# A quarter of the Q projection as seven-product runs on shared row sums, with the PSUM ring turned by two

## The chip, the cores and the metric

One core of one Trainium2 chip. The time is device time in microseconds (us), the median of several executions. "Before" is the kernel as it stood, "after" the changed one. A profile is taken of one of the executions, and stage times are read from it.

In this kernel TensorE makes the matrix products. A product lies in a bank of PSUM (128x512 floats) until ScalarE or VectorE has read it, and the program waits for these reads before it writes the bank again. A transfer between memories is called a DMA; a queue holds those that one engine has issued.

## The reference

```python
def _A_ref(x, wqkv, wo):                    # B, S, D = 1, 2048, 1024; 32 heads of 32
    q, k, v = ...(x @ wqkv)
    phi = lambda t: jnp.where(t > 0, t + 1, jnp.exp(t)) + 1e-6
    pq, pk = phi(q), phi(k)
    kv = jnp.einsum("bhsd,bhse->bhde", pk, v)
    z = jnp.einsum("bhsd->bhd", pk)
    num = jnp.einsum("bhqd,bhde->bhqe", pq, kv)
    den = jnp.einsum("bhqd,bhd->bhq", pq, z)[..., None] + 1e-6
    return (num / den)... @ wo
def _B_ref(x, w1, b1, w2, b2):              # mixes over the rows: w1 2048x3584, w2 3584x2048
    ...
h = x + _A_ref(_layernorm(x), A_wqkv, A_wo)
h2 = h + _B_ref(_layernorm(h), B_w1, B_b1, B_w2, B_b2)
```

The change lies in `_A_ref`, which the kernel finishes at about 234 us. The rest, the two mixers of `_B_ref`, it doesn't touch.

## The kernel before

The row-normalised x is kept transposed in `xnT` (8 k tiles of 128 partitions). K and V are made in runs that cover two row tiles each. A run takes a 2x2 block product by seven block products (`p1` to `p7`) instead of eight. It needs sums of x blocks (`x_sums`, shared by the K and the V run of the same rows) and of weight blocks (`w_sums`, made once). The runs interleave, so that VectorE and ScalarE work on one while TensorE makes the next.

```python
def x_sums(q):
    a11, a12, a21, a22 = x_blocks(q)
    sm = spool.tile([P, 4, hk2, P], FP16, tag="xs", name="xs")      # two buffers
    pin(nc.vector.tensor_tensor(sm[:, 0], a21, a22, ALU.add))
    ...
class Run:
    def mm(self, ps, lhs, rhs, start):
        for k in range(hk2):                                        # 4 matmuls of 512 columns
            pin(nc.tensor.matmul(ps[:], lhsT=lhs[:, k, :], rhs=rhs[:, k, :], ...))
    def p7(self):
        self.mm(self.C, self.s3, self.t3, False)
        self.add(1, self.C)          # VectorE reads psC
    def p4(self):
        self.mm(self.C, self.a22, self.t4, False)   # TensorE goes on in psC
        self.evac(1, self.C)
    ...
def run_step(n, prev, ...):          # the next run's products between the last run's
    n.p1(); ...; prev.p3(); ...; prev.p4(); n.p6(); ...; n.p2(); n.p5(); ...
```

Q is made in plain units of 8 matmuls of 512 columns, 32 of them. Eight lie between the runs, the other 24 in the "held" stage, beside the folding of `kv` into `wo`, the denominators and the first sums of mixer 1. A denominator row is inverted by ScalarE into a buffer `rd` and sent through DRAM, to be spread over partitions.

```python
q_units = [(u, j) for u in range(NSC) for j in range(ND)]           # 4 x 8
def den_inv(u, ps):
    rd = a3d.tile([P, SW], FP16, tag="rd", name="rd")               # one buffer
    hs.activation(ps[:], ps[:], ACT.Ln, bias=eps_den[:], scale=1.0 / S)
    hs.activation(rd[:], ps[:], ACT.Exp, scale=-1.0)                # hs: ScalarE
    hd.dma_start(rd_dram[u][:], rd[:])
...
for n, (u, j) in enumerate(q_units[8:]):
    q_held(u, j)
    if 4 <= n < 4 + ND:
        fold(n - 4)
    if j == 1:                                                      # every 8 units
        den(u - 1)
        den_spread(u - 1)
    ...
```

Plain units, folds and output tiles take their PSUM bank in turn from a ring of five:

```python
acc_ring[:] = [acc, pool, acc, pool, pool][0:2 + bufs]
def acc_tile():
    acc_ring.append(acc_ring.pop(0))
    return acc_ring[-1].tile([P, BANK], F32, tag="acc", name="acc_t")
```

## Time and profile before

| | before |
|---|---|
| median (range), 3 runs | 560.21 us (560.14 to 560.31) |
| span of the profiled execution | 558.3 us |
| first V run to held stage | 100.46 us |
| held stage, 24 Q units | 47.40 us |
| output stage, up to mixer 1 | 55.90 us |
| mixer 1 to the end | 324.4 us |

The stage lengths are differences of four starts in the timeline of TensorE of the kernel before (start us, length us, engine, line, operation, out<-in, tile, count). They are the first product of the first V run, the first held Q unit, the first output tile and the first product of mixer 1:

```profile
30.11 1.03 PE L946 MATMUL psA<-wkv,xnT 128*128 128x512 bf16 x4
...
130.57 1.67 PE L230 MATMUL acc_t<-xnT,wq_sb 128*128 128x512 bf16 x7
...
177.97 2.32 PE L230 MATMUL acc_t<-wo_sb,pqT 128*128 128x512 f16 x10
...
233.87 2.32 PE L230 MATMUL psA<-hE,wq 128*128 128x512 f16 x10
```

(The end of the span is read to 0.1 us.)

### The profile page before, as it was taken

Reading aid. Unit: us, or ns where it says so; the run is one execution under the profiler, and the core shown is the slowest. Engines: PE = TensorE matmul, PEld = TensorE weight load, DVE = VectorE, ACT = ScalarE, POOL = GpSimd, SP = SyncE. Lnnn points to the kernel's source line nnn. Section 1 sums busy time; section 2 is a strip of 40 time slices with the busy share of each in tenths; the row PEclk is TensorE's granted clock in tenths of the full one; section 3 lists DMA queues with packets and bytes.
Section 4 is the critical chain, followed back from the end, with each engine's and each line's share of the span. In section 5 each row is a group of like instructions: output and inputs, shape, how many; then the busy total and the mean of one; then the engine's idle time right before and its main releaser. Section 6 shows DMA issues by size and latency. Waiting matters only on the chain.

```text
span 558.3 us, 8814 instructions
## 1 busy us (share of the span) xinstructions
PE 551.9 (99%) x3323; PEld 315.8 (57%) x3339; DVE 436.1 (78%) x850; ACT 291.0 (52%) x617; POOL 26.3 (5%) x36
## 2 busy tenths in 40 slices
PE   8999999999999999999999999999999999999997
PEld 3444444454444444456766767667444667767665
DVE  7898888544777688889989889897996878749746
ACT  5747677766767877645455565464310312413312
POOL 1000000000000000000000000000003103103111
PEclk9999999999999999999999999999999999999999
DMA  9933342115764772102240430413769649849434
GB/s 300 304 75 76 82 89 39 19 39 201 224 202 138 239 205 76 75 1 79 75 150 3 150 126 26 151 40 94 197 209 236 195 125 244 214 129 239 93 108 73
DMA packets 83915, 74.51 MB, mean 133 GB/s; under 512 B 15634, under 2 KB 76320, under 8 KB 83872
## 3 DMA queue, kind: packets, MB, share of 16 engines
q1 hardware_dynamic: 79104, 69.61, 41.9%
q0 software_dynamic: 4096, 3.68, 4.8%
q10 hardware_dynamic: 672, 0.66, 0.3%
q8 instruction: 26, 0.43, 0.3%
q14 instruction: 17, 0.14, 0.1%
HBM read 59.12 MB, written 11.67 MB: 127 GB/s over the span
## 4 chain that ended last, share of the span: by engine, by line
PE 95%; DMA 2%; DVE 2%; issue 1%; ACT 0%; DVEq 0%
PE psI L230 25%; PE acc_t L230 18%; PE psC L230 16%; PE psB L230 8%; PE psC L946 4%; PE psB L946 4%; PE psA L946 4%; PE psB L342 2%; PE psA L342 2%; PE acc_t L1232 2%; PE psE L946 2%; DMA x_sb<-in_A_x_dram 2%; PE psC L342 2%; PE acc_t L870 2%; PE psA L230 1%; PE kvps L899 1%
## 5 line engine op out<-in xcount | busy, mean ns | idle before, releaser
L230 PEld LDWEIGHTS <-is 128*128 128x128 f16 x736 | 71.9, 98 | 31.1 <-DVE hi L230 0.4
L230 PEld LDWEIGHTS <-sa 128*128 128x128 f16 x606 | 59.2, 98 | 27.1
L230 PEld LDWEIGHTS <-wq 128*128 128x128 bf16 (+1 forms) x496 | 48.5, 98 | 28.1 <-issue 1.0
L230 PE MATMUL acc_t<-wo_sb,pqT 128*128 128x512 f16 x256 | 55.6, 379 | 0.0
L488 POOL DMA_DIRECT2D out_dram<-wq x28 | 24.4, 928 | 519.8 <-ACT wq L491 489.5
L230 PE MATMUL acc_t<-xnT,wq_sb 128*128 128x512 bf16 x188 | 43.1, 379 | 0.2
L230 PEld LDWEIGHTS <-pqT 128*128 128x128 bf16 x256 | 25.0, 98 | 30.5 <-issue 0.6
L193 DVE TENSOR_SCALAR e_sb<-e_sb 128x512 bf16<-128x512 bf16 x64 | 18.6, 290 | 28.7 <-ACT e_sb L189 28.2
L230 DVE TENSOR_TENSOR t<-psI,t 128x256 f32<-128x256 f32 (+1 forms) x45 | 20.8, 475 | 22.2 <-PE psI L230 20.9
L189 ACT ACTIVATE e_sb<-acc_t 128x512 bf16<-128x512 f32 x40 | 23.9, 597 | 24.5 <-PE acc_t L230 12.0
L230 PE MATMUL psC<-gs,wq 128*128 128x512 f16 x140 | 34.1, 379 | 0.0
L946 PEld LDWEIGHTS <-xs 128*128 128x128 f16 x208 | 20.0, 98 | 23.4 <-DVE xs L932 1.3
L230 PEld LDWEIGHTS <-wq_sb 128*128 128x128 bf16 x192 | 18.5, 98 | 23.0 <-issue 1.3
L230 PE MATMUL psC<-hT,sa 128*128 128x512 f16 x112 | 31.2, 379 | 0.0
L230 PE MATMUL psI<-hi,is 128*128 128x256 f16 x200 | 30.0, 273 | 0.0
L230 PE MATMUL psB<-hT,sa 128*128 128x512 f16 x112 | 29.7, 379 | 0.0
L230 DVE BATCH_NORM_STATS2 hst<-acc_t 128x6 f32<-128x512 f32 x32 | 21.4, 692 | 9.0 <-ACT h_bf L230 8.9
L946 PE MATMUL psA<-wkv,xnT 128*128 128x512 bf16 x99 | 26.4, 379 | 0.3
L946 PEld LDWEIGHTS <-xnT 128*128 128x128 bf16 x156 | 15.2, 98 | 18.5 <-issue 0.2
L230 PE MATMUL psC<-hT,wq 128*128 128x512 f16 x96 | 24.6, 379 | 0.0
L230 ACT CAST h_bf<-acc_t 128x512 bf16<-128x512 f32 x32 | 18.4, 582 | 11.9 <-PE acc_t L230 11.5
L230 ACT COPY psI<-psI 128x256 f32<-128x256 f32 x50 | 18.0, 360 | 11.6 <-PE psI L230 9.7
(229 smaller groups left out, 1089.6 us busy)
## 6 DMA issues: line engine op xcount, KB each, us to landing
wq<-in_B_w_dram SPq DMA_DIRECT2D x14, 1024.0 KB, 7.8
wq<-in_B_w_dram SPq DMA_DIRECT2D x12, 896.0 KB, 7.2
gs<-parked SPq DMA_DIRECT2D x9, 896.0 KB, 4.7
xr<-in_A_x_dram SPq DMA_DIRECT2D x16, 256.0 KB, 5.3
rdb<-rd_dram SPq DMA_DIRECT2D x32, 128.0 KB, 3.8
out_dram<-h_bf SPq DMA_DIRECT2D x16, 256.0 KB, 2.0
x_sb<-in_A_x_dram SPq DMA_DIRECT2D x15, 256.0 KB, 3.0
w2o<-in_B_w_dram SPq DMA_DIRECT2D x4, 896.0 KB, 10.7
```

The costliest lines, as they stand in the source:

```text
L189: pin(nc.scalar.activation(e_sb[:], src, ACT.Exp))
L193: pin(nc.vector.tensor_scalar(e_sb[:], e_sb[:], 1.0, PHI_EPS, ALU.min, ALU.add))
L230: return (lambda *a, **kw: pin(op(*a, **kw))) if self.always or getattr(Held, self.key) else op
L342: pe.matmul(ps[:, cols], lhsT=lhs[:, k, :], rhs=mv(k)[:, cols], start=(start and k == 0), stop=(k == self.nk - 1), skip_group_check=True,)
L488: nc.gpsimd.dma_start(to, ot[:, a:b], accum_op=ALU.add)
L870: mm = nc.tensor.matmul(pp[:, 0:CW], lhsT=xnT[:, kt, i * P:(i + 1) * P], rhs=wkv[:, kt, c * CW:(c + 1) * CW], start=(kt == 0), stop=(kt == ...
L899: pin(nc.tensor.matmul(kv_ps[b][:, sl, :], lhsT=pks[i % NPK][:, j * P:(j + 1) * P], rhs=vaugs[i % NVA][:, j, :], start=False, stop=(i == N ...
L946: pin(nc.tensor.matmul(ps[:], lhsT=lhs[:, k, :], rhs=rhs[:, k, :], start=(start and k == 0), stop=(k == hk2 - 1), skip_group_check=True,))
L1232: nc.tensor.matmul(qp[:, 0:SW], lhsT=wq_sb[:, kt, j * P:(j + 1) * P], rhs=xnT[:, kt, u * SW:(u + 1) * SW], start=(kt == 0), stop=(kt == ND ...
```

## The change

Its intent is to stream fewer columns through TensorE. The eight plain units of u = 2 (rows 1024 to 1535) become two Q runs of seven products, one on each side of V run 5. They use x sums that K and V make anyway, with x as the moving operand and the sums of Wq as the stationary one. The held stage keeps 16 units, so its folds, denominators and scalings move closer together. The `rd` buffer, the spread rows, some sums of Wk and Wq and the first x rows now share one region (`shared_sb`). Half of mixer 1's first weights is loaded earlier, and the ring is turned by two tiles, since eight tiles fewer would give mixer 1's first product another bank.

```diff
+            qmov = [wq_b[:, :, k, :, c, :] for k in range(2) for c in range(2)], tq
...
+            class QRun(KRun):
+                def mm(self, ps, lhs, rhs, start):
+                    out = ps[:].rearrange("p (j r f) -> p j r f", j=2, f=P)
+                    for j in range(2):
+                        for k in range(hk2):
+                            pin(nc.tensor.matmul(
+                                out[:, j],
+                                lhsT=rhs[:, k, 2 * self.half + j, :],
+                                rhs=lhs[:, k],                  # 2 x 128 columns, with a gap
...
-            q_units = [(u, j) for u in range(NSC) for j in range(ND)]
+            q_units = [(u, j) for u in (0, 1, NSC - 1) for j in range(ND)]
...
+                if q == 5:
+                    runs = [runs[0], QRun(q // 2, 0), runs[1], QRun(q // 2, 1)]
...
+                        if kind == "K" and q in q_sums:          # q = 2..5, one sum each
+                            w_sums(qmov, q_sums[q])
...
-                rd = a3d.tile([P, SW], FP16, tag="rd", name="rd")
-                hs.activation(rd[:], ps[:], ACT.Exp, scale=-1.0)
-                hd.dma_start(rd_dram[u][:], rd[:])
+                hs.activation(rd_sb, ps[:], ACT.Exp, scale=-1.0)  # rd_sb: still one buffer
+                hd.dma_start(rd_dram[u][:], rd_sb)
...
+            for half in range(2):
+                load_w1(0, half, pin)                            # ahead of the x rows
             for i in range(XRL + 1):
                 load_xr(i)
...
+            for _ in range(2):
+                acc_ring.append(acc_ring.pop(0))
...
-                if j == 1:
-                    den(u - 1)
-                    den_spread(u - 1)
+                if n in den_at:                                  # {0: 0, 2: 2, 9: 1}
+                    den(den_at[n])
+                if n in spread_at:                               # {0: 0, 6: 2, 12: 1}
+                    den_spread(spread_at[n])
```

More of the change, by code (lines that the diff above doesn't have):

```diff
@@ L182, in combine, with phi_parts @@
             v.tensor_tensor(t4, o[:, lo], t2, sub)
-    def phi_parts(dst, src, n, pool):
+    def phi_parts(dst, src, n, pool, view=lambda t: t, lean=False):
         e_sb = pool.tile([P, n], BF16, tag="phi_e", name="e_sb")
-        r_sb = pool.tile([P, n], BF16, tag="phi_r", name="r_sb")
+        r_sb = None if lean else pool.tile([P, n], BF16, tag="phi_r", name="r_sb")
         def act():
             pin(nc.scalar.activation(e_sb[:], src, ACT.Exp))
-            pin(nc.scalar.activation(r_sb[:], src, ACT.Relu))
+            if not lean:
+                pin(nc.scalar.activation(r_sb[:], src, ACT.Relu))
         def dve():
             pin(nc.vector.tensor_scalar(e_sb[:], e_sb[:], 1.0, PHI_EPS, ALU.min, ALU.add))
-            pin(nc.vector.tensor_tensor(dst, e_sb[:], r_sb[:], ALU.add))
+            if lean:
+                pin(nc.vector.scalar_tensor_tensor(dst, view(src), 0.0, view(e_sb[:]), ALU.max, ALU.add))
+            else:
+                pin(nc.vector.tensor_tensor(dst, view(e_sb[:]), view(r_sb[:]), ALU.add))
         return act, dve
@@ L781 @@
         a3s = actx.enter_context(tc.tile_pool(name="a3s", bufs=4))
-        a3d = actx.enter_context(tc.tile_pool(name="a3d", bufs=1))
         hstat = actx.enter_context(tc.tile_pool(name="hstat", bufs=1))
-        xrpool = actx.enter_context(tc.tile_pool(name="xrpool", bufs=XRL + 1))
+        QT = ND // 2 * CW
+        shared_sb = hstat.tile([P, 3 * QT + SW + (XRL + 1) * D], BF16, name="shared_sb")
+        thirds = [shared_sb[:, i * QT:(i + 1) * QT] for i in range(3)]
+        rd_sb = shared_sb[:, 3 * QT:3 * QT + SW].bitcast(FP16)
+        xr_at = 3 * QT + SW
+        xr_first = [shared_sb[:, xr_at + i * D:xr_at + (i + 1) * D] for i in range(XRL + 1)]
+        assert (XRL + 1) * D >= 2 * QT
         mv_all = hstat.tile([P, NS, nc.vector.BN_AGGR_DIM], F32)
@@ L809 @@
             pks = [a1w.tile([P, D], BF16, name=f"pk{t}") for t in range(NPK)]
-            tv = wo_sb[:].rearrange("p (t a) (b c) -> p t (a b) c", t=4, c=CW).bitcast(FP16)
-            tk = pqT[:, ND - 4:ND, :].rearrange("p t (b c) -> p t b c", c=CW).bitcast(FP16)
-            spool = a1.enter_context(tc.tile_pool(name="spool", bufs=2))
+            tv = [
+                t.bitcast(FP16).rearrange("p (k c) -> p k c", c=CW)
+                for t in (wo_sb[:, 2 * t:2 * t + 2, :].rearrange("p a b -> p (a b)") for t in range(4))
+            ]
+            later = [pqT[:, j:j + 4, u * SW:(u + 1) * SW].bitcast(FP16) for u, j in ((1, 0), (NSC - 1, 0), (NSC - 1, 4))]
+            tk = [t.bitcast(FP16).rearrange("p (k c) -> p k c", c=CW) for t in thirds] + [later[0]]
+            tq = [
+                t.bitcast(FP16).rearrange("p (k j f) -> p k j f", k=ND // 2, f=P)
+                for t in (shared_sb[:, xr_at:xr_at + QT], shared_sb[:, xr_at + QT:xr_at + 2 * QT])
+            ] + [t.rearrange("p k (j f) -> p k j f", f=P) for t in later[1:]]
+            spool = a1.enter_context(tc.tile_pool(name="spool", bufs=1))
             e1pool = a1.enter_context(tc.tile_pool(name="e1pool", bufs=1))
@@ L912, in w_blocks @@
                 return w[:, :, 0, 0:CW], w[:, :, 0, CW:D], w[:, :, 1, 0:CW], w[:, :, 1, CW:D]
-            kmov = w_blocks(0), tuple(tk[:, t] for t in range(4))
-            vmov = w_blocks(D), tuple(tv[:, t] for t in range(4))
+            wq_b = wq_sb[:].rearrange("p (k two) (j par f) -> p k two j par f", two=2, par=2, f=P)
+            kmov = w_blocks(0), tk
+            vmov = w_blocks(D), tv
+            qmov = [wq_b[:, :, k, :, c, :] for k in range(2) for c in range(2)], tq
             def w_sums(mov, part):
@@ L920, in w_sums @@
                     pin(nc.vector.tensor_tensor(out, a, b, ALU.subtract))
-            xsum = {}
+            xs_sb = spool.tile([P, 2, 4, hk2, P], FP16, name="xs")
             def x_blocks(q):
@@ L926, in x_blocks, with x_sums @@
                 return v[:, :, 0, 0, :], v[:, :, 1, 0, :], v[:, :, 0, 1, :], v[:, :, 1, 1, :]
-            def x_sums(q):
+            def x_sums(q, part=slice(0, 4)):
                 a11, a12, a21, a22 = x_blocks(q)
-                sm = spool.tile([P, 4, hk2, P], FP16, tag="xs", name="xs")
-                pin(nc.vector.tensor_tensor(sm[:, 0], a21, a22, ALU.add))
-                pin(nc.vector.tensor_tensor(sm[:, 1], sm[:, 0], a11, ALU.subtract))
-                pin(nc.vector.tensor_tensor(sm[:, 2], a11, a21, ALU.subtract))
-                pin(nc.vector.tensor_tensor(sm[:, 3], a12, sm[:, 1], ALU.subtract))
-                xsum[q] = sm
+                sm = xs_sb[:, q % 2]
+                for out, a, b, op in (
+                    (sm[:, 0], a21, a22, ALU.add), (sm[:, 1], sm[:, 0], a11, ALU.subtract),
+                    (sm[:, 2], a11, a21, ALU.subtract), (sm[:, 3], a12, sm[:, 1], ALU.subtract),
+                )[part]:
+                    pin(nc.vector.tensor_tensor(out, a, b, op))
             class Run:
@@ L940, in __init__ @@
                     self.a11, self.a12, self.a21, self.a22 = x_blocks(q)
-                    self.s1, self.s2, self.s3, self.s4 = (xsum[q][:, t] for t in range(4))
+                    self.s1, self.s2, self.s3, self.s4 = (xs_sb[:, q % 2, t] for t in range(4))
                     (self.b11, _, self.b21, self.b22), (self.t1, self.t2, self.t3, self.t4) = mov
@@ L1027, in __init__, with view @@
                     self.phi = {}
+                lean = False
+                def view(self, t):
+                    return t
                 def dst(self, h, c):
@@ L1032, in evac @@
                 def evac(self, h, ps):
-                    self.phi[h, 0] = phi_parts(self.dst(h, 0), ps[:], CW, a2k)
+                    self.phi[h, 0] = phi_parts(self.dst(h, 0), ps[:], CW, a2k, self.view)
                     self.phi[h, 0][0]()
@@ L1038, in add @@
                     pin(nc.vector.tensor_tensor(t[:], ps[:], self.E[:], ALU.add))
-                    self.phi[h, 1] = phi_parts(self.dst(h, 1), t[:], CW, a2k)
+                    self.phi[h, 1] = phi_parts(self.dst(h, 1), t[:], CW, a2k, self.view, self.lean)
                 def late12(self):
@@ L1057, in dve22, with __init__, view, dst @@
                     self.phi[1, 1][1]()
-            def run_step(n, prev, after6=None, after5=None, after7=None, fill=None):
+            class QRun(KRun):
+                lean = True
+                def __init__(self, u, half):
+                    self.u, self.half, self.phi = u, half, {}
+                    xv = xnT[:, :, u * SW:(u + 1) * SW].rearrange("p (k two) (r t f) -> p k two r t f", two=2, t=2, f=P)
+                    self.a11, self.a12, self.a21, self.a22 = (xv[:, :, k, :, t, :] for t in range(2) for k in range(2))
+                    self.s1, self.s2, self.s3, self.s4 = (
+                        xs_sb[:, :, t].rearrange("p r k f -> p k r f") for t in range(4)
+                    )
+                    (self.b11, _, self.b21, self.b22), (self.t1, self.t2, self.t3, self.t4) = qmov
+                def view(self, t):
+                    return t.rearrange("p (j n) -> p j n", j=2)
+                def mm(self, ps, lhs, rhs, start):
[6 more added lines that the diff above has]
+                                rhs=lhs[:, k],
+                                start=(start and j == 0 and k == 0),
+                                stop=(k == hk2 - 1),
+                                skip_group_check=True,
+                            ))
+                def dst(self, h, c):
+                    n0 = self.u * SW + h * SW // 2
+                    v = pqT[:, 4 * self.half:4 * self.half + 4, n0:n0 + SW // 2]
+                    return v.rearrange("p (j two) n -> p j two n", two=2)[:, :, c, :]
+            def run_step(n, prev, after6=None, after5=None, after7=None, fill=None, after3=None):
                 if n is not None:
@@ L1065, in run_step @@
                 prev.p3()
+                if after3 is not None:
+                    after3()
                 prev.dve22()
@@ L1078, in run_step @@
                     n.dve11()
-                prev.dve12()
+                behind = QRun in (type(n), type(prev))
+                if not behind:
+                    prev.dve12()
                 if after5 is not None:
@@ L1083, in run_step @@
                     n.p7()
+                if behind:
+                    prev.dve12()
                 if after7 is not None:
@@ L1239, in q_unit @@
                 phi_evac(pqT[:, j, u * SW:(u + 1) * SW], qp[:, 0:SW], SW, a2k)
-            q_units = [(u, j) for u in range(NSC) for j in range(ND)]
+            assert NSC == 4
+            q_units = [(u, j) for u in (0, 1, NSC - 1) for j in range(ND)]
             NVP = NS // 2
@@ L1268 @@
             prev = v1
+            q_sums = {2: slice(0, 1), 3: slice(1, 2), 4: slice(2, 3), 5: slice(3, 4)}
             for q in range(2, NVP):
-                for R in (KRun, VRun):
-                    n = R(q)
-                    i = 2 * q + 3 if R is KRun else 2 * q + 4
+                runs = [KRun(q), VRun(q)]
+                if q == 5:
+                    runs = [runs[0], QRun(q // 2, 0), runs[1], QRun(q // 2, 1)]
+                for n in runs:
+                    kind = type(n).__name__[0]
+                    i = {"K": 2 * q + 3, "V": 2 * q + 4}.get(kind, NS)
+                    if q == 5 and kind == "Q":
+                        i = NS - 1 if n.half == 1 else NS
+                    elif q == 6 and kind == "K":
+                        i = NS
                     def after6():
@@ L1278, in after5 @@
                     def after5():
-                        if R is VRun:
+                        if kind == "V":
                             kv_accum(2 * q - 2)
@@ L1286, in after7, with after3 @@
                     def after7():
-                        if R is VRun and q + 1 < NVP:
+                        if kind == "V" and q != 5 and q + 1 < NVP:
                             x_sums(q + 1)
-                    run_step(n, prev, after6, after5, after7)
+                        if kind == "Q" and n.half == 1:
+                            x_sums(q + 1, slice(0, 3))
+                        if kind == "K" and q in q_sums:
+                            w_sums(qmov, q_sums[q])
+                    def after3():
+                        if type(prev) is QRun and prev.half == 1:
+                            x_sums(q, slice(3, 4))
+                    run_step(n, prev, after6, after5, after7, after3=after3)
                     prev = n
@@ L1347 @@
             rdbs = {}
+            SPREAD = (0, 2, 1, 3)
             NH = ND // 2
@@ L1374, in den_spread @@
                 for h in range(2):
-                    rdb = a3d.tile([P, NH, SW], FP16, tag="rdb", bufs=3, name="rdb")
+                    rdb = thirds[(2 * SPREAD.index(u) + h) % 3].bitcast(FP16).rearrange("p (j n) -> p j n", n=SW)
                     for q in range(HB):
@@ L1387, in scale_q @@
                 v = pqT[:, h * NH:(h + 1) * NH, u * SW:(u + 1) * SW]
-                hv.tensor_tensor(v, v, rdbs.pop((u, h))[:], ALU.mult)
+                hv.tensor_tensor(v, v, rdbs.pop((u, h)), ALU.mult)
             def q_held(u, j):
@@ L1407, in load_xr @@
                 if i < NS:
-                    pool = xr2pool if XRL < i <= XRL + XR2 else xrpool
-                    xr = pool.tile([P, D], BF16, name="xr")
-                    hd.dma_start(xr[:], x[i * P:(i + 1) * P, :])
+                    if XRL < i <= XRL + XR2:
+                        xr = xr2pool.tile([P, D], BF16, name="xr")[:]
+                    else:
+                        xr = xr_first[i % (XRL + 1)]
+                    hd.dma_start(xr, x[i * P:(i + 1) * P, :])
                     xrs[i] = xr
@@ L1418, in seed, with place @@
                         hs.copy(seeds[i][dc][:, 0:CW], xr[:, dc * CW:(dc + 1) * CW])
+            def place(i):
+                u, r = divmod(i, NSC)
+                return i if u != 2 else NSC * u + r % 2 * 2 + r // 2
             def out_mm(i):
+                at = place(i) * P
                 for dc in range(NDC):
@@ L1424, in out_mm @@
                             seeds[i][dc][:, 0:CW],
-                            lhsT=pqT[:, j, i * P:(i + 1) * P],
+                            lhsT=pqT[:, j, at:at + P],
                             rhs=wf[:, j, dc * CW:(dc + 1) * CW],
@@ L1470, in first_sums @@
                 yield cur
-            sums_at, ahead = (11, 13, 17, 19, 21), first_sums()
-            scale_at = {7: (0, 0), 8: (0, 1), 15: (1, 0), 16: (1, 1), 23: (2, 0)}
+            for _ in range(2):
+                acc_ring.append(acc_ring.pop(0))
+            sums_at, ahead = (4, 8, 9, 11, 13), first_sums()
+            scale_at = {5: (0, 0), 6: (0, 1), 10: (2, 0), 12: (2, 1), 15: (1, 0)}
+            den_at = {0: 0, 2: 2, 9: 1}
+            spread_at = {0: 0, 6: 2, 12: 1}
+            kv_transpose()
             for n, (u, j) in enumerate(q_units[8:]):
@@ L1477 @@
                 q_held(u, j)
-                if 4 <= n < 4 + ND:
-                    fold(n - 4)
-                if j == 1:
-                    den(u - 1)
-                    den_spread(u - 1)
-                if n == 2:
-                    kv_transpose()
-                if n in (4, 5, 10, 11):
-                    load_w1(n // 10, n % 2, pin)
+                if 1 <= n < 1 + ND:
+                    fold(n - 1)
+                if n in den_at:
+                    den(den_at[n])
+                if n in spread_at:
+                    den_spread(spread_at[n])
+                if n in (12, 13):
+                    load_w1(1, n % 2, pin)
                 if n in scale_at:
@@ L1500 @@
             hT4 = hpool.tile([P, NSP, CW], FP16, name="hT4")
-            scale_at = {0: (NSC - 2, 1), 6: (NSC - 1, 0), 8: (NSC - 1, 1)}
+            scale_at = {0: (1, 1), 6: (3, 0), 8: (3, 1)}
             for i in range(NS):
```

## The prediction

> **What bounds the kernel now.** I read the page first (busy shares, then the chain that ended last), then what TensorE waited for, then the windows of the stages that the change touches, then the order of instructions inside them.
>
> ```profile
> PE 551.9 (99%) x3323; PEld 315.8 (57%) x3339; DVE 436.1 (78%) x850; ACT 291.0 (52%) x617; POOL 26.3 (5%) x36
> PE 95%; DMA 2%; DVE 2%; issue 1%; ACT 0%; DVEq 0%
> ```
>
> TensorE is busy for 551.9 of 558.3 us and the chain that ended last is TensorE for 95%. That alone doesn't prove a bound, since matmul ends are modelled, so I looked for its waits. The view of waits has three lines for it, 1.7 us in all, and all lie before 35 us (the longest is 1.2 us at the very start). The windows say the same for the stages of this change (columns: length, then busy us of PE, PEld, DVE, ACT, POOL, then granted clock, DMA share, GB/s):
>
> ```profile
> 41.00:119.27 78.27, 77.96 (x428) 38.47 (x433) 58.20 (x133) 58.15 (x118) 0.00 (x0) 1.00 0.26 55
> 130.57:177.97 47.40, 47.19 (x238) 20.93 (x240) 31.49 (x69) 34.80 (x65) 0.00 (x0) 1.00 0.60 180
> 177.97:233.87 55.90, 55.90 (x265) 25.08 (x264) 45.02 (x92) 40.65 (x96) 0.00 (x0) 1.00 0.47 149
> ```
>
> The first is the K and V runs, the second the 24 held Q units with the folds, the third the output projection. TensorE is full in each (the odd 0.1 us are matmul records that the trace lacks: groups of 8 show as x7), and VectorE and ScalarE are 66 to 81% busy. So the kernel moves here only with the number of columns that TensorE streams, or if the change makes it wait.
>
> The price of a column, from the order of time on TensorE around two Q units and inside the second mixer (start, length, then what):
>
> ```profile
> 119.27 1.89 PE L1232 MATMUL acc_t<-xnT,wq_sb 128*128 128x512 bf16 x7
> 120.99 1.03 PE L946 MATMUL psB<-wkv,xs 128*128 128x512 bf16 x4
> ...
> 432.51 0.93 PE L230 MATMUL psI<-gi,is 128*128 128x256 f16 x7
> 433.27 0.93 PE L230 MATMUL psI<-gE,wq 128*128 128x256 f16 x7
> 434.04 1.67 PE L230 MATMUL psC<-gs,wq 128*128 128x512 f16 x7
> ```
>
> Starts are what counts, not lengths: the page's 379 ns of one matmul overlaps the next. A Q unit is 8 matmuls of 512 columns; start to start that is 1.72 to 1.73 us (5.18 us for the three units from 125.39 to 130.57), so 215.8 ns each. Fourteen of 256 columns take 434.04 - 432.51 = 1.53 us, so 109.3 ns each.
>
> **What the Trainium skill says.** "TensorE: Matmul & The Clock Gate", section "Wait — 56ns, not 53.3ns?", gives the warm start-to-start as N / 2.4 GHz plus about 2.5 ns: 215.8 ns at 512 and 109.2 at 256, as the trace has it. "VectorE: DVE Perf Modes", section "Mode 2×_1P — pack two bf16 into one 32-bit read", lets a tensor_tensor of adjacent 16-bit elements make two results a cycle; at 0.96 GHz 2048 elements are then 1.07 us, and the trace's 128x2048 sums take 1.22, so about 0.15 is fixed cost. The new weight sums have runs of 128 adjacent elements, as the mixer's sums have, so I price them at 1.22. "PSUM — Partial Sum Buffer", section "Summary: rules for kernel authors", says to guard PSUM by bank: hence a tile that reuses a bank must wait for the last reader of that bank, which is what the turned ring is about. The same page ("Specifications (TRN2)") warns that a non-contiguous PSUM pattern slows matmuls. The Q runs write 256 adjacent columns, so it should not bite; no matmul that I looked at in this trace has such a gap to try it on.
>
> **The change part by part.**
>
> *Removed.* Eight Q units (u = 2): 64 matmuls of 512, 64 x 215.8 ns = 13.81 us of TensorE in the held stage, with eight evacuations.
>
> *Added on TensorE.* Two QRuns, each seven products of 8 matmuls (2 column groups x 4 k) of 256 columns: 112 x 109.3 ns = 12.24 us between K5 and V6. Each matmul loads its own weights; a load takes 98 ns, under the 109 ns of a matmul, as in the mixers' inner runs, so loads stay hidden. Columns fall from 32768 to 28672, seven eighths. Net -1.57 us, all on the path.
>
> *Added on VectorE.* Four sums of Wq, one behind each K run from q = 2 to 5, 4 x 1.22 = 4.9 us. The X sums come free, since K and V already make them. A QRun has two adds from PSUM (0.69), four clamps (0.29), two adds (0.42) and two fused relu-adds on float data (estimate 0.74, from the mixer's fused operation of that size): 4.9 us, 9.7 for both. The stage then has 58.2 + 4.9 + 9.7 = 72.8 us in 78.3 + 12.2 = 90.5, 80%.
>
> *Added on ScalarE.* Three copies (0.57), four passes on PSUM (0.60), two on the float sum (0.63): 5.4 us a run against 6.1 us of TensorE; the stage becomes (58.2 + 10.7) / 90.5 = 76%.
>
> So no engine fills up; the order within a step matters more. The tightest place is a V step, where VectorE gets a 1.22 us sum and must still deliver the next X sums to product 6 of the next K run. VectorE in the V step from 47.1 us:
>
> ```profile
> 48.09 0.69 DVE L1038 TENSOR_TENSOR kt<-psC,e 128x512 f32<-128x512 f32 x1
> 49.06 0.69 DVE L1038 TENSOR_TENSOR kt<-psB,e 128x512 f32<-128x512 f32 x1 [0.28 <-PE psB L946]
> ...
> 52.69 0.21 DVE L842 BATCH_NORM_AGGREGATE mv<-st 128x2 f32<-128x12 f32 x1
> 53.66 0.29 DVE L193 TENSOR_SCALAR e_sb<-e_sb 128x512 bf16<-128x512 bf16 x1 [0.76 <-ACT e_sb L189]
> ```
>
> The sum goes in behind 48.09. Idle time there: 0.28, a 0.19 between the two lines, and 0.76 before ScalarE's late exp at 53.66: 1.23 us. A sum costs 1.22 less the 0.09 by which neighbours overlap. It fits with 0.1 us to spare, so I expect the X sums on time, or at worst 0.1 to 0.3 us late in three V steps. In the Q steps the postponed `dve12` brings the add that TensorE needs ahead of work that it doesn't.
>
> *Moved.* The held stage falls from 47.4 to about 33.6 us and keeps folds, denominators, scalings and mixer 1's sums. VectorE: 31.5 less 8 x 0.65 = 26.3, ScalarE 34.8 less 8 x 1.09 = 26.1, both 78% of 33.6. Five PSUM banks and four buffers of exp results give slack of several units. Transfers: wo, half of w1 and x rows are now 5 MB in one queue, where wo and x (3 MB) took from about 124 to 132 us, at 368 GB/s. I estimate 14 us for 5 MB, done some 9 us into the stage; the first denominator rows then arrive by 13 to 16 us, and VectorE reaches their first use at about 16. Close, but a VectorE wait there of a us or two is hidden behind the banks.
>
> *The turn of the ring.* Eight tiles fewer change the position modulo 5. Counting, before: 1 + 24 + 16 + 32 = 73 tiles, and mixer 1's first product gets the bank of the second half of output tile 13. With 65 tiles and no turn it would get the first half of the last output tile, whose statistics are read until 234.35 us, while the product starts at 233.87: a wait of about 0.5 us or somewhat more. Turned, it gets the second half of tile 14, free since 232.2. So the turn gains nothing against before; it prevents a loss. I expect no wait there.
>
> Sum: 560.21 - 1.57 = 558.64; 0 to 0.3 us for small new waits; I say 558.7.
>
> **Rivals.** (1) The moving operand of a QRun is two pieces of 128 elements with a gap, where all moving operands before are one piece. If a gap costs, say, 10 ns a matmul, 112 of them take back 1.1 us (time 559.8); 20 ns would make it slower, 560.9. Against: the stride is long but the pieces are whole; nothing in the profile tests it. (2) VectorE becomes the bound of the K and V stage: the X sums come late and TensorE waits at each of three or four K runs, perhaps 0.3 to 0.5 us each: 559.7 to 560.3. For: only 0.1 us spare; against: the idle time before the late exp takes it up. (3) The shortened held stage is bound by transfers or VectorE, and a late scaling stalls the banks: up to 2 us lost, 560.5. Against: 22% idle on both engines and the early w1. (4) More than the columns is gained: the trace has under 0.3 us of waits in this region, so no better than 558.2.
>
> **Range and chances.** The arithmetic is firm; nearly all rivals make it slower than 558.6. So the range is lopsided: 558.0 to 560.2. The bound of 2% is 11.2 us either way, seven times the effect: within 2% is nearly certain, 0.98; faster 0.01, slower 0.01.
>
> **What would show it.** Right: the 112 new matmuls at 109 ns start to start (0.87 us a product); the first held unit about 12.2 us later than 130.57; the output stage 1.5 us earlier than 177.97, mixer 1 as much before 233.87, the two stages unchanged in length from there; TensorE's waits no more than before. Wrong: products of a QRun over 0.9 us, gaps before loads from `xs` at the start of K runs 3 to 6, TensorE waiting for ScalarE or VectorE between K5 and V6, a wait of VectorE for a DMA at the first scaling followed by a gap on TensorE, or a wait before mixer 1's first product.

## More of the kernel before

The next two lines are from ScalarE's timeline of the kernel before and matter only with hindsight. They are the first two writes of the single `rd` buffer:

```profile
135.90 0.60 ACT L230 ACTIVATE rd<-den_ps 128x512 f16<-128x512 f32 x1
...
153.46 0.60 ACT L230 ACTIVATE rd<-den_ps 128x512 f16<-128x512 f32 x1
```

They are 17.6 us apart and neither has a wait noted behind it. The row had long been sent when the buffer was written again.

## The result, and the profile after

After: **559.97 us** median of 4 runs (559.27, 559.48, 560.45, 561.02). Before on the same chip: 560.26 (560.14 to 560.67). The ratio is 0.9995, 95% interval 0.9976 to 1.0014: the same within 2%, inside the predicted range, but 1.3 us above the predicted 558.7.

The page of the kernel after, busy time of each engine and the chain that ended last:

```profile
PE 550.3 (98%) x3370; PEld 320.7 (57%) x3387; DVE 442.7 (79%) x858; ACT 291.7 (52%) x619; POOL 26.2 (5%) x36
...
PE 93%; DMA 2%; DVE 2%; ACT 1%; SPq 1%; issue 1%; DVEq 0%; ACTq 0%
```

TensorE is busy 1.6 us less, as the columns say, yet the span of this execution grew from 558.3 to 558.7 us. So some 2 us of waiting came in. The four starts again, from the timeline of TensorE of the kernel after (the held stage now opens with a transpose of `kv`):

```profile
31.62 1.03 PE L965 MATMUL psA<-wkv,xnT 128*128 128x512 bf16 x4
...
144.32 0.61 PE L234 MATMUL acc_t<-ident,kvbd 128*128 128x128 bf16 x8
...
178.38 1.89 PE L234 MATMUL acc_t<-wo_sb,pqT 128*128 128x512 f16 x8
...
234.28 3.62 PE L234 MATMUL psA<-hE,wq 128*128 128x512 f16 x16
```

| stage | before | after | expected from the columns | surplus |
|---|---|---|---|---|
| start of the first V run | 30.11 | 31.62 | 30.11 | +1.51 |
| V run to held stage, now with the Q runs | 100.46 | 112.70 | 100.46 + 12.24 = 112.70 | 0.00 |
| held stage | 47.40 | 34.06 | 47.40 - 13.81 = 33.59 | +0.47 |
| output stage | 55.90 | 55.90 | 55.90 | 0.00 |
| mixer 1 to the end | 324.4 | 324.4 | 324.4 | 0.0 |

The two surpluses make 1.98 us, more than the 1.57 that the columns save.

**The opening.** TensorE's timelines, first the kernel before, then the kernel after, at the first projection matmuls:

```profile
7.06 1.47 PE L870 MATMUL acc_t<-wkv,xnT 128*128 128x512 bf16 x6
```

```profile
8.56 1.45 PE L887 MATMUL acc_t<-wkv,xnT 128*128 128x512 bf16 x6 [1.75 <-DMA wkv<-in_A_wqkv_dram]
```

In the brackets stands how long the engine sat idle and what ended it. The first weights came late. One of their loads, issued at 1.18 us by ScalarE's queue, took 7.2 us to land here and 4.7 us in the kernel before. The change doesn't touch this part: the order of the loads and the addresses of x, of `xnT` and of the weights in the built programs are the same in both kernels. So chance of this one execution was my first suspect.

**The Q runs.** Their products, from the timeline of TensorE of the kernel after:

```profile
90.34 1.04 PE L1102 MATMUL psB<-xs,shared_sb 128*128 128x256 f16 x8
91.21 1.04 PE L1102 MATMUL psA<-xnT,wq_sb 128*128 128x256 bf16 x8
92.09 1.04 PE L1102 MATMUL psE<-xs,shared_sb 128*128 128x256 f16 x8
```

Eight matmuls start to start take 0.87 us, 109 ns each, as one-piece operands of 256 columns do in the second mixer. The gap in the moving operand costs nothing. The three stages, in the view of windows of the kernel after (columns as in the prediction):

```profile
42.51:133.01 90.50, 90.08 (x537) 49.55 (x544) 70.77 (x157) 67.88 (x136) 0.00 (x0) 1.00 0.23 47
144.32:178.38 34.06, 33.74 (x174) 14.66 (x176) 25.17 (x52) 25.91 (x49) 0.00 (x0) 1.00 0.67 193
178.38:234.28 55.90, 55.90 (x265) 25.07 (x264) 45.35 (x94) 40.64 (x96) 0.00 (x0) 1.00 0.56 185
```

VectorE has 70.8 us in the first (I had worked out 72.8) and 25.2 in the held stage (26.3). ScalarE has 67.9 (68.9) and 25.9 (26.1).

**The tight V step.** VectorE's timeline of the kernel after, the step that the prediction shows of the kernel before:

```profile
49.60 0.68 DVE L1062 TENSOR_TENSOR kt<-psC,e 128x512 f32<-128x512 f32 x1
50.20 1.22 DVE L939 TENSOR_TENSOR shared_sb<-wq_sb 128x2048 f16<-128x2048 bf16 x1
51.34 0.68 DVE L1062 TENSOR_TENSOR kt<-psB,e 128x512 f32<-128x512 f32 x1
...
55.18 0.29 DVE L194 TENSOR_SCALAR e_sb<-e_sb 128x512 bf16<-128x512 bf16 x1 [0.25 <-ACT e_sb L189]
```

The 1.22 us sum went in, and VectorE still waits 0.25 us for ScalarE's exp further on. The late exp comes at the same place in the step as before: 5.58 us after the first line here, 5.57 in the kernel before.

**The held stage.** ScalarE's timeline of the kernel after has one wait that the kernel before lacks, at the second write of the denominator buffer:

```profile
154.81 0.60 ACT L234 ACTIVATE shared_sb<-den_ps 128x512 f16<-128x512 f32 x1 [1.45 <-DMA rd_dram<-shared_sb]
```

And TensorE's timeline of the same moment, a fold between two Q units:

```profile
154.27 1.89 PE L234 MATMUL acc_t<-xnT,wq_sb 128*128 128x512 bf16 x8
156.00 0.81 PE L234 MATMUL acc_t<-wo_sb,kvT 128*128 128x512 bf16 x2
156.91 1.89 PE L234 MATMUL acc_t<-xnT,wq_sb 128*128 128x512 bf16 x8
```

From one unit to the next it takes 2.64 us. The pair before it (a start at 152.10, the next at 154.27) took 2.17. The difference is the 0.47. The denominators of u = 0 and u = 2 are now two units apart instead of eight, and both go through one buffer. The first row was issued at 148.99 and released the buffer about 5.8 us later; in the kernel before such a row took 1.7 us from issue to landing (median of two). Issued ahead of it in the same queue, from 136.44 us on, are `wo`, half of w1 and the x rows, 5 MB. The Trainium skill says in "DMA: Bandwidth & Descriptors", section "Queues, rings and completion order", that the sync engine has one ring on each of the 16 DMA engines, and that descriptors are taken from a ring in order, though a later one may finish before an earlier one. The trace agrees as far as it goes: the transfer rate stays at 350 to 384 GB/s from 138 us until about 152.5 us, and only after that is the buffer free. ScalarE, which stands waiting, does not empty the PSUM banks of the Q units and folds, and TensorE soon has to wait for one. This trace names no releaser for that gap; the runs below do.

### The profile page after: what moved, and what is told of

Its sections match the earlier page's. It is cut to its first block, busy times and chain, and to the rows that moved or that the text cites. A ratio compares the mean times of both kernels' runs of the same rounds, so it can differ in the third digit from the quotient of the medians.

```text
span 558.7 us, 8921 instructions
## 1 busy us (share of the span) xinstructions
PE 550.3 (98%) x3370; PEld 320.7 (57%) x3387; DVE 442.7 (79%) x858; ACT 291.7 (52%) x619; POOL 26.2 (5%) x36
## 4 chain that ended last, share of the span: by engine, by line
PE 93%; DMA 2%; DVE 2%; ACT 1%; SPq 1%; issue 1%; DVEq 0%; ACTq 0%
PE psI L234 25%; PE psC L234 16%; PE acc_t L234 14%; PE psB L234 8%; PE psC L965 4%; PE psB L965 4%; PE psA L965 4%; PE psB L346 2%; PE psA L346 2%; PE acc_t L1295 2%; PE psE L965 2%; PE psC L346 2%; PE acc_t L887 2%; DMA x_sb<-in_A_x_dram 1%; PE psA L234 1%; PE kvps L916 1%
## 5 line engine op out<-in xcount | busy, mean ns | idle before, releaser
L234 PE MATMUL acc_t<-xnT,wq_sb 128*128 128x512 bf16 x125 | 29.3, 379 | 0.3
L189 ACT ACTIVATE e_sb<-acc_t 128x512 bf16<-128x512 f32 x32 | 19.1, 598 | 18.6 <-PE acc_t L1295 10.0
L234 DVE TENSOR_TENSOR e<-psI,es 128x256 f32<-128x256 f32 x20 | 8.5, 425 | 19.9 <-PE psI L234 17.8
```

The lines of the kernel that those rows point to most:

```text
L189: pin(nc.scalar.activation(e_sb[:], src, ACT.Exp))
L234: return (lambda *a, **kw: pin(op(*a, **kw))) if self.always or getattr(Held, self.key) else op
```

## The experiments

Ten kernels ran, all with a correct result, in three sets, each on one chip: the first four of the second table, the next four, the last two. Each has five timed runs, beside nine of the kernel before for the set. Stage lengths are from their profiles (us).

| run | first V run | to held stage | held | output | rest | span |
|---|---|---|---|---|---|---|
| before | 30.11 | 100.46 | 47.40 | 55.90 | 324.4 | 558.3 |
| after | 31.62 | 112.70 | 34.06 | 55.90 | 324.4 | 558.7 |
| after_again | 30.32 | 112.70 | 34.03 | 55.91 | 324.4 | 557.4 |
| xr_late | 30.01 | 112.69 | 33.58 | 55.90 | 324.5 | 556.7 |
| two_rd | 30.26 | 112.69 | 33.59 | 55.90 | 324.4 | 556.8 |
| no_turn | 30.18 | 112.69 | 34.36 | 57.57 | 324.3 | 559.1 |
| both | 30.35 | 112.69 | 33.58 | 55.90 | 324.4 | 556.9 |
| before_again | 30.31 | 100.46 | 47.40 | 55.90 | 324.4 | 558.5 |
| q_eight | 30.49 | 114.44 | 34.25 | 55.90 | 325.0 | 560.1 |
| sums_twice | 30.17 | 114.55 | 34.23 | 55.90 | 325.1 | 559.9 |
| after_third | 30.49 | 112.69 | 34.07 | 55.90 | 324.4 | 557.5 |
| after_fourth | 30.38 | 112.68 | 33.89 | 55.90 | 325.0 | 557.8 |

| run | median (range) | before in the same set | ratio, 95% interval |
|---|---|---|---|
| after_again | 559.19 (559.04 to 559.78) | 560.33 | 0.9982, 0.9970 to 0.9995 |
| xr_late | 558.68 (558.43 to 559.00) | 560.33 | 0.9973, 0.9960 to 0.9985 |
| two_rd | 559.13 (558.61 to 559.85) | 560.33 | 0.9983, 0.9969 to 0.9996 |
| no_turn | 561.28 (560.90 to 562.74) | 560.33 | 1.0025, 1.0012 to 1.0037 |
| both | 558.78 (558.53 to 559.58) | 560.28 | 0.9971, 0.9958 to 0.9983 |
| before_again | 560.26 (560.17 to 560.30) | 560.28 | 0.9994, 0.9982 to 1.0007 |
| q_eight | 561.87 (561.58 to 562.45) | 560.28 | 1.0024, 1.0011 to 1.0038 |
| sums_twice | 561.76 (560.99 to 561.98) | 560.28 | 1.0019, 1.0007 to 1.0032 |
| after_third | 559.32 (559.06 to 559.80) | 560.26 | 0.9982, 0.9968 to 0.9995 |
| after_fourth | 559.51 (559.14 to 560.75) | 560.26 | 0.9986, 0.9973 to 0.9998 |

By the bound of 2% all of them are the same as before. What is read from them below is smaller, and rests on the stages of the profiles first.

### after_again: the changed kernel once more

No edit.

> The changed kernel once more, nothing altered. Theory A (the gain of 1.57 us is there, but the profiled run lost 1.5 us in its opening, where TensorE waited for the first K weights until 8.56 us against 7.06, and 0.47 us in the held Q stage): the opening is a matter of chance in each execution, so over five rounds the times scatter by more than 1 us and the mean lies about 1.1 us under before (ratio 0.998); in the profile the stretch from the first V product to mixer 1's first product is again 202.6 to 202.7 us against 203.76 before. Theory B (the change itself delays the opening, through other addresses or a longer program): the opening ends near 8.5 us in this profile too, and the mean is within 0.4 us of before in all rounds. Theory C (Q runs cost more than they save): the stretch is 203.7 us or longer.

The first V run starts at 30.32 us, and the 34.03 us of the held stage are back. So the late opening doesn't belong to the changed kernel as such, while the held stage's surplus does. With both in the account, 560.33 - 1.57 + 0.44 = 559.20 us; the median is 559.19.

### xr_late: the x rows later

```diff
-            for i in range(XRL + 1):
-                load_xr(i)
...
             for n, (u, j) in enumerate(q_units[8:]):
                 ...                             # after den_spread
+                if n == 0:
+                    for i in range(XRL + 1):
+                        load_xr(i)
```

> The first four loads of x rows for the residual are issued behind the first spread of the denominators, not ahead of it; all else as changed. In the changed kernel ScalarE waits 1.45 us at 153.4 until the first denominator rows have left the one buffer that the second also uses; those rows wait in the queue behind wo, w1 and the x rows (5 MB). Theory A (that queue makes the wait, and the wait makes TensorE's gap of 0.47 us in the fourth fold): with 1 MB less ahead the rows leave about 2.5 us earlier, the ScalarE wait goes, the held stage falls from 34.06 to 33.6 us, the kernel gains 0.4 to 0.5 us on the changed one. Rival (VectorE's mixer sum or its backlog makes the gap): the wait of ScalarE goes but the held stage stays at 34.0.

One MB less lies ahead of the first denominator row. ScalarE waits for no transfer in the held stage, which falls to 33.58 us. The time is 0.51 us under after_again, and the five runs of the one lie wholly below the five of the other.

### two_rd: another buffer for the second row

```diff
-                hs.activation(rd_sb, ps[:], ACT.Exp, scale=-1.0)
-                hd.dma_start(rd_dram[u][:], rd_sb)
+                rd = thirds[2][:, 0:SW].bitcast(FP16) if u == 2 else rd_sb
+                hs.activation(rd, ps[:], ACT.Exp, scale=-1.0)
+                hd.dma_start(rd_dram[u][:], rd)
```

> The second denominator (u = 2) gets its own buffer in a third that is free, the transfers stay in their order. Theory A: ScalarE's 1.45 us wait for the rows that leave goes, TensorE's gap in the fourth fold goes, held stage 33.6 us instead of 34.06, 0.4 to 0.5 us faster than the changed kernel; the spread still starts at about 10.4 us into the stage, as the queue is unchanged. If the late transfer itself (not the shared buffer) makes the gap, the stage stays at 34.06.

The transfers stay as they were and only the shared buffer goes. ScalarE's and TensorE's timelines of this kernel at the same moment:

```profile
152.03 0.60 ACT L234 ACTIVATE shared_sb<-den_ps 128x512 f16<-128x512 f32 x1
```

```profile
152.91 1.89 PE L234 MATMUL acc_t<-xnT,wq_sb 128*128 128x512 bf16 x8
154.63 0.59 PE L234 MATMUL acc_t<-wo_sb,kvT 128*128 128x512 bf16 x2
155.07 1.89 PE L234 MATMUL acc_t<-xnT,wq_sb 128*128 128x512 bf16 x8
```

No wait, 2.16 us from unit to unit, and 33.59 us for the stage: exactly what the columns need. So the late row costs nothing unless its buffer is written again; xr_late shows that the reuse costs nothing unless the row is late. The expected gain of 0.4 to 0.5 us doesn't show in the times: 559.13 against 559.19. One of its five runs is at 559.85 for reasons that no trace covers.

### both: the two cures together

> The changed kernel with both cures of the held stage: the third denominator row in a spare buffer (as in two_rd) and the x rows loaded after the first spread (as in xr_late). Each alone took the held stage from 34.06 to 33.58 us, which is what TensorE's columns alone need (33.59). Theory (both cure the same wait): nothing is left to gain, held stage 33.5 to 33.7 us, median 558.5 to 559.1. Rival (they cure different parts): the stage comes under 33.4 us or the median under 558.3.

33.58 us and 558.78 us: the two cure the same wait, and nothing more lies there.

### no_turn: the ring not turned

```diff
-            for _ in range(2):
-                acc_ring.append(acc_ring.pop(0))
```

> The changed kernel without the turn of the PSUM ring. My account of the banks: mixer 1's first product then takes the bank of the first half of the last output tile, whose statistics VectorE reads until about 0.5 us after TensorE has finished the output. Expected: a wait of TensorE of 0.4 to 0.7 us before psA's first matmul, released by VectorE's statistics, and 0.4 to 0.7 us more time than the changed kernel (ratio to before up by 0.001). If the turn is worth nothing, no wait and the same time; then the allocator gives another bank than I count.

Without the turn the kernel is slower than the one before. VectorE's timeline, then TensorE's, at the start of mixer 1:

```profile
233.95 0.70 DVE L234 BATCH_NORM_STATS2 hst<-acc_t 128x6 f32<-128x512 f32 x1 [0.33 <-ACT h_bf L234]
```

```profile
234.80 3.61 PE L234 MATMUL psA<-hE,wq 128*128 128x512 f16 x16 [1.50 <-DVE hst L234]
```

The output stage is 1.67 us longer start to start. The statistics that the product waits for are those of the **second** half of the last tile, which end at 234.65. I had expected the first half and half a microsecond. The bank numbers of the built kernels settle it: with the turn, mixer 1's first product takes the bank of the first half of output tile 14; without it, that of the second half of tile 15, the last. I had miscounted the order in which the ring's banks come. The five runs scatter more than usual (560.90 to 562.74), and only one was profiled.

### before_again: the kernel before once more

> The kernel before, unedited, for a second profile of its opening. Theory (the 1.5 us by which the first profile of the changed kernel started its K and V runs late are chance of one execution, in whatever kernel): the first V product's psA starts within 30.0 to 30.4 us here, as in four of the five profiles of changed kernels and the one of before; median 560.0 to 560.7, ratio 1.000. Stages from there as in the first profile of before: 100.46 us to the held stage, 47.40 us held, 55.90 us output, each within 0.1.

All stages up to mixer 1 are as in the first profile to 0.01 us and the opening ends at 30.31 us. Of twelve profiles, six of them of the two unedited kernels, only the first one after the change started late.

### q_eight: one product made twice

```diff
             class QRun(KRun):
+                def p1(self):
+                    self.A = vps.tile([P, BANK], F32, tag="va", name="psA")
+                    self.mm(self.A, self.a11, self.b11, True)
+                    self.mm(self.A, self.a11, self.b11, True)
+                    self.B = acc.tile([P, BANK], F32, tag="acc", name="psB")
+                    pin(nc.scalar.copy(self.B[:], self.A[:]))
```

> The changed kernel with the first product of each Q run made twice (the second time over the first, so the result stays right): 16 more matmuls of 256 columns, with which the Q runs stream as many columns as the eight plain units did. Theory (TensorE's columns alone price the Q runs): 16 x 109.3 ns = 1.75 us more, first V product to held stage 114.45 us instead of 112.70, median 1.6 to 1.9 us over that of after_again (559.19), so 560.8 to 561.1. Rival (VectorE or ScalarE set the pace of a Q run): less than 1 us more. If the sum comes out just above the kernel before, the whole gain is the missing eighth product less the wait in the held stage.

To the held stage it takes 114.44 us, 1.74 more, as expected to 0.01. The Q runs cost what TensorE streams and nothing else. The median missed its range by 0.8 us for other reasons, which the profile shows against after_again: 0.17 us in the opening, 0.22 in the held stage (ScalarE waited 1.63 us there, not 1.42) and 0.6 behind the start of mixer 1. The last goes with a weight load of mixer 2 that came late, in VectorE's timeline of this kernel:

```profile
474.07 0.63 DVE L234 TENSOR_TENSOR is<-wq 128x896 f16<-128x896 bf16 x1 [0.58 <-DMA wq<-in_B_w_dram]
```

### sums_twice: every sum of Wq made twice

```diff
                         if kind == "K" and q in q_sums:
                             w_sums(qmov, q_sums[q])
+                            w_sums(qmov, q_sums[q])
```

> The changed kernel with every sum of Wq made twice, so 1.13 to 1.22 us more VectorE work in each of the V steps behind K runs 2, 3, 4 and 5; the result stays right. Theory (the prediction's 0.1 us to spare in a V step is real): after the one sum VectorE still idles 0.25 and 0.23 us in the step, so the X sums come 0.65 to 1.1 us late at the sixth product of K runs 3, 4 and 5 (behind run 5 the X sums follow a Q run, so less there): 2.0 to 3.3 us in all, median 561.2 to 562.6, gaps on TensorE before the loads from xs. Rival (more slack than was counted, for instance because the product's bank wait hides it): under 0.5 us in all, median under 559.7.

TensorE waits in three V steps, and the runs take 1.85 us longer, a little less than my range. But it does not wait where I said. VectorE's timeline of this kernel, then TensorE's:

```profile
48.75 2.48 DVE L939 TENSOR_TENSOR shared_sb<-wq_sb 128x2048 f16<-128x2048 bf16 x2
51.14 0.68 DVE L1062 TENSOR_TENSOR kt<-psB,e 128x512 f32<-128x512 f32 x1
```

```profile
55.05 1.03 PE L965 MATMUL psB<-wkv,xs 128*128 128x512 bf16 x4
56.53 1.02 PE L965 MATMUL psC<-wo_sb,xnT 128*128 128x512 f16 x4 [0.46 <-DVE vaug L1036]
```

The wait is at `p4`, which goes on in psC and so needs VectorE's add from psC first. That add stands ahead of the x sums and is due one product earlier. Start to start the step is 1.48 us instead of 0.86, so 0.62 late, and three times 0.62 is the 1.85. The second sum pushed VectorE's next add back by 1.25 us (2.39 us from sum to add here, 1.14 in the kernel after). Of that, 0.63 us was absorbed: this is the slack that was left in the step after the first sum, six times the 0.1 us of the prediction. The median, 561.76, fell in its range, but with help from another late weight load of mixer 2 (0.62 us at 513 us).

### after_third and after_fourth: how far single executions scatter

No edit in either.

> The changed kernel, unedited, a third profile. Theory (the first profile's opening, 1.5 us late on a weight load, was chance; the steady cost of the change is the 0.47 us in the held stage): first V product's psA at 30.0 to 30.5 us, 112.7 us to the held stage, 34.0 to 34.1 us held, median 559.0 to 559.5 us, 1.0 to 1.2 below the kernel before, and single runs up to 0.6 higher where a weight load of mixer 2 lands late. Rival (the changed kernel itself has two openings): psA at 31 us or more in this profile or the next, or run times in two groups 1.5 us apart.

> As after_third: a fourth profile of the changed kernel. Theory: psA at 30.0 to 30.5 us, held stage 34.0 to 34.1 us, median 559.0 to 559.5 us. Rival (two openings): psA at 31 us or more, or run times in two groups 1.5 us apart.

The openings end at 30.49 and 30.38 us. The rival, a second kind of opening, has no further case in a profile; the run times don't fall into two groups either, though one run of after_fourth, 560.75 us, stands 1.2 us above its other four and has no trace. The median of after_fourth, 559.51, is at the edge of the range. Its held stage, 33.89 us, is a little under the range, with a ScalarE wait of 1.27 us instead of 1.45. It also has the late weight load of mixer 2, in VectorE's timeline and then TensorE's:

```profile
511.30 0.62 DVE L234 TENSOR_TENSOR is<-wq 128x896 f16<-128x896 bf16 x1 [0.52 <-DMA wq<-in_B_w_dram]
```

```profile
520.56 2.10 PE L234 MATMUL psB<-gT,sa 128*128 128x512 f16 x9 [0.18 <-ACT psB L531]
```

VectorE's 0.5 us reach TensorE nine microseconds later, by way of ScalarE: this product starts 287.71 us into mixer 1, against 287.14 in after_again, and the rest of the execution is 0.6 us longer. Three of the twelve profiles have this, in kernels whose mixers are all alike. It would explain single runs half a microsecond above their neighbours, which have no trace. Why some executions have it is open.

**All waits of the held stage together.** Seven profiles have the wait for the buffer. Beside each is the surplus of its held stage over 33.59 us:

| | fourth | again | after | third | sums_twice | q_eight | no_turn |
|---|---|---|---|---|---|---|---|
| ScalarE waits for the buffer | 1.27 | 1.42 | 1.45 | 1.45 | 1.61 | 1.63 | 1.75 |
| surplus of the stage | 0.30 | 0.44 | 0.47 | 0.48 | 0.64 | 0.66 | 0.77 |
| difference | 0.97 | 0.98 | 0.98 | 0.97 | 0.97 | 0.97 | 0.98 |

The banks and buffers hide 0.97 us of this wait; what is longer, up to the 1.75 us seen, reaches TensorE in full. In no_turn, which has the longest, the gap in the fourth fold is wide enough for TensorE's timeline to name what ended it (q_eight and sums_twice have the same with 0.2 us):

```profile
155.28 0.38 PE L234 MATMUL acc_t<-wo_sb,kvT 128*128 128x512 bf16 x1 [0.36 <-ACT r_sb L191]
```

`r_sb` is ScalarE's second pass over a Q unit in PSUM. So TensorE waits for ScalarE to read a bank.

## Why the prediction was right, and where it failed

**Right: the price of the columns.** The 112 matmuls at 109.3 ns came to the predicted 12.24 us, the 64 removed ones to 13.81. two_rd and q_eight confirm both signs to 0.01 us. The transfer into the total is one to one, as the full TensorE of the view of windows suggested.

**Right: rivals 1 and 2 don't happen.** The gap in the moving operand is free (0.87 us a product). VectorE is in time, and with more room than I counted. I had set the sum's 1.13 us against the idle time in the step as I listed it and got 0.1 us; the chip absorbed another 0.63 us before TensorE waited. The step also has waits for ScalarE behind the late exp. And the sums_twice run shows that the first thing due is not the x sums but the add that frees psC.

**Failed: "a VectorE wait there of a us or two is hidden behind the banks".** This is the step on the held stage, rival 3, whose cost in the sum was "0 to 0.3 us for small new waits". A wait in this stage cost 0.44 to 0.48 us in three profiles and 0.30 in the fourth. I had the late denominator rows right (5 MB ahead of them in one queue), but followed them only to their reader, VectorE at the scaling. VectorE starts the first scaling 17 us into the stage (161.29 us in the kernel after) and waits there for no DMA, so the wait that I named never came. What waited was their *writer*: ScalarE, because the next row goes into the same buffer, and its spacing had shrunk from eight units to two. ScalarE reads every Q unit from PSUM, and every other fold tile. Of its wait the banks hide 0.97 us, not two; how much of a VectorE wait they would hide, no run here shows.

**Failed, without consequence for the time: the turn of the ring.** I predicted no wait with the turn, and there is none. Its worth I put at 0.5 us; it is 1.67, since I had the wrong half of the last tile.

**Not foreseen: chance.** The first profiled execution lost 1.51 us in the opening to a late weight load. Another run of that set was slow too (561.02 us), but was not profiled, so its cause stays open. The kernel before has such runs too: 561.57 and 561.46 us among its nine of the second set, with a median of 560.28, also without a trace. Two of the four first runs, 560.45 and 561.02, lie above the predicted range. That the median of 559.97 lies inside it is partly luck: the range reached up to 560.2 for the sake of rivals 1 to 3, and what lengthened the profiled run most is a late load that none of them names. The three later medians of the same kernel, 559.19 to 559.51, lie 0.75 to 1.14 us under before, against 1.57 predicted and about 1.1 expected with the held stage's wait. The remainder is of the size of mixer 2's late load in some of the runs; that this is the cause is argued, not shown.

The three kernels without the held stage's wait are xr_late (558.68 us), both (558.78) and two_rd (559.13). They lie 1.65, 1.50 and 1.20 us under the kernel before in their sets, where the columns make 1.57. The first two have the time that the prediction named; two_rd's profiled run, its fastest, has it too (558.61); what lengthened its other four no trace shows.

## What to carry to other kernels

When a stage is shortened, look at each buffer with a single copy in it: count how far apart its writes now are, how long its reader, a DMA too, holds it, and what lies ahead of that DMA in its queue. Follow a late transfer to both ends, to whoever reads the data and to whoever must write the source again. For changes of a microsecond or two, compare starts of stages inside the profiles of several executions: here those without a stray wait agree to 0.02 us, while whole runs of one kernel differ by up to 1.8 us (no_turn).

## What the Trainium skill lacked or had wrong

- "Advanced Engine Details and Errata", section "Memory Cachelines", warns of accesses that go to a new SBUF line each time but gives no figure for a matmul operand in pieces. Here a moving operand of two pieces of 128 adjacent 16-bit elements ran at 109 ns for 256 columns, the same as one piece. The warning about non-contiguous PSUM patterns was not tried; the outputs were adjacent.
- "DMA: Bandwidth & Descriptors" has the order within a ring, but I found no example there of what it does to a small transfer. A row of 128 KB took 1.7 us from issue to landing (median of two) in a quiet queue, and kept its source buffer for about 5.8 us behind the rest of 5 MB of loads.
- No page that I found says how much waiting of the engine that empties PSUM five banks can hide. In this stage it was 0.97 us, in seven profiles to 0.01.
